# Keys' scores in four tiles that later hold the left tiles' sets; tables spread by products of ones; low parts by GpSimd

## The chip, the cores and the metric

The kernel runs on one core of a Trainium2 chip. A core has a matrix engine (TensorE, here PE, with its weight loads shown apart as PEld), and the engines VectorE (DVE), ScalarE (ACT) and GpSimd (POOL). SyncE (SP) issues most transfers; POOL issues the indirect ones. Each engine takes its instructions in the order in which they were written into its queue. The metric is device time in microseconds, the median of several runs.

## The reference

```python
def _attn_ref(q, k, v, agents):
    scale = 1.0 / np.sqrt(q.shape[-1])
    def sm(a, b):
        s = scale * (a @ b.transpose(0, 2, 1))
        s = s - s.max(-1, keepdims=True)
        e = np.exp(s)
        return e / (e.sum(-1, keepdims=True) + 1e-09)
    a2k = sm(agents, k)
    agent_v = a2k @ v
    q2a = sm(q, agents)
    return q2a @ agent_v
...
    logits = x @ w_gate
    e_idx = np.argmax(logits, axis=1)
...
    for e in range(E):
        mask = e_idx == e
        h = np.maximum(x[mask] @ w1[e], 0.0)
        ye = h @ w2[e]
        out[mask] = gate_w[mask, None] * eom[mask, e, None] * ye
```

q, k and v have shape (4, 11456, 128), and there are 49 agents per batch. The result of the attention, 45824 rows of 128, goes through a layer of 8 experts with 1024 hidden values, each row through the expert of its largest logit. Its output is scaled by that expert's probability and an output gate.

## The kernel before, in words

Each of the 4 batches is cut into 12 units: eleven of 1024 tokens (8 columns of 128) and one of 192. For keys, PE forms scores of a unit against the agents (`ks`), ACT copies them to `S`, DVE keeps a running maximum (`mx`), then POOL subtracts the maximum, ACT takes the exponential (`ev`) and PE adds up the agents' values from `v`.

The output of the attention is never formed for most tokens. The kernel folds the agents' values of a batch into the first weights of the one expert that takes most of this batch's tokens (`fold`, `first`), so that the softmax numerators of q (49 values and their low parts, `x1`, `x2`) are multiplied by 128-row weights `w` at once. This main stream runs over 92 tiles of up to 512 tokens. For each, PE makes eight blocks of hidden values `h` (two groups of four banks), ACT applies the relu and rounds to half precision (`hh`), DVE forms what was rounded away (`hl`), and PE multiplies both by `vv` into `y`. ACT (`ys`) and DVE (`os`) add up `y`, POOL scales it, and SP stores it to `out`.

Scores of q are taken in half precision from high and low parts. `split` makes these: ACT squares the unit for a norm, a product of ones and `scale` give a power of two, ACT writes the high part `xh`, DVE the low part `xl`. The units in `WHOLE` (all keys, the first eight units of batch 0, all of batch 3) are multiplied in single precision instead and pass no split, so 28 units do.

Tokens whose expert is not the batch's main one are the left tokens. Per phase (batches 0 to 2, then batch 3) `q_tail` stores running counts (`cumd`), and `left_table` makes a table of left tiles of 128 tokens: 13 of phase 0, one of phase 1. In this text a left tile is also called a set; `left_index` handles a group of sets at a time: from the table's rows (`tb`, `ti`) and the prefix rows (`pb`) it works out addresses, gathers the counts of `cumd` by indirect transfers on POOL, works out the tokens, and gathers their attention numerators from `efd`. `left_static`, in two interleaved ways, loads the expert's weights, then PE transposes the numerators (`let`), multiplies them by the agents' values (`lx`), and by the two weights in single precision (`lh`, relu, `ly`); `left_scatter` writes over the rows of `out`.

Before the change the tables go through memory: `left_table` stores them (`ttd`, `ttid`, `ppid`), and `left_index` loads them back, spread over all partitions, with a register read on SP for each set. `left_prepare` takes one phase after the other (groups of 2, 3, 3 and 5, then 1); the groups' buffers are the tile of `cum`, two load buffers, and the one tile of `S`, and none is begun before all of batch 3's key weights are summed.

The order of instructions on each queue is made when the program is written: a clock with costs for each operation (`Clock`, `Engine.cost`) decides in which order the generators started with `spawn` are advanced; a smaller second argument is served first. A change of engine or cost in one place thus reorders others. L204 is the line of the helper that writes every instruction.

Of the kernel before, what the change touches and what calls it, by code (L numbers as in the profile page):

```python
# [9 lines left out]
I32 = mybir.dt.int32  # L10
# [243 lines left out]
def agent_attention_top1_moe(ctx, tc, qT, kT, v, aT, wg, wo, w1, w2, cst, out):  # L254
# [158 lines left out]
    def split(item):  # L413
# [3 lines left out]
        while item not in parts or splits[0] - scored_n[0] > 1:  # L417
# [14 lines left out]
                                        op1=ALU.mult)  # L432
        yield from ACT.q.activation(xh[:, 0:n], x[:, 0:n], AF.Copy, scale=s)
        xl = x.bitcast(F16)
        yield from DVE.q.scalar_tensor_tensor(xl[:, 0:n], x[:, 0:n], s, xh[:, 0:n], op0=ALU.mult, op1=ALU.subtract)
# [188 lines left out]
    def k_unit(b, u):  # L624
        if u == 0:
            K[b] = dict(
                S=wk.tile([P, NCOL, A2], F32, name=f"S{b}", tag="S", bufs=1),
                mx=wk.tile([P, 8, A2], F32, name=f"mx{b}", tag="mx", bufs=1),
                sm=wk.tile([P, 8, A2], F32, name=f"sm{b}", tag="sme", bufs=1),
                k=0, s=0, v=0, av_n=0,  # L630
            )
        s, mark, inv = yield from scores(("k", b, u), f"ks{b}_{u}")
        spawn(k_rest(b, u, s, mark, inv))

    def k_rest(b, u, s, mark, inv):
# [5 lines left out]
        Su = S[0:pp, 8 * u:8 * u + nt, :]  # L641
# [5 lines left out]
        if u > 0:  # L647
            yield from DVE.q.tensor_tensor(mx[0:pp, 0:nt], Su, S[0:pp, 0:nt, :] if u == 1 else mx[0:pp, 0:nt],
                                           op=ALU.max)
# [14 lines left out]
    def v_weights(b, u):  # L664
# [3 lines left out]
        sv = S[0:pp, 8 * u:8 * u + nt, :]  # L668
# [572 lines left out]
    def left_table(ph):  # L1241
# [5 lines left out]
        def row(n, w=NG, dt=F32):  # L1247
            return lt(n, [w], f"_{ph}", [min(w, ng)], dt)
# [22 lines left out]
        ppt = lt("pptsb", [P], f"_{ph}", [P])  # L1271
# [15 lines left out]
        ni = a0  # L1287
        yield from DVE.q.tensor_copy(nti[ph], ni[:, ng - 1:ng])

        yield from DVE.q.tensor_scalar(over[:, ph:ph + 1], ni[:, ng - 1:ng], float(PHASES[ph][2]), None, op0=ALU.is_gt)  # L1290
        tt = lt("tt", [4, 8], f"_{ph}", [kr, 8])
# [16 lines left out]
        yield from low_bits(tt[:, :, 3], g_, E - 1, lt("g_i", [4], f"_{ph}", [kr], I32))  # L1308
        yield from DVE.q.tensor_tensor(ne, g_, tt[:, :, 3], op=ALU.subtract)
        yield from DVE.q.tensor_scalar(tt[:, :, 4], ne, 1.0 / E, None, op0=ALU.mult)  # L1310
# [3 lines left out]
        yield from SY.q.dma_start(ttid[ph].rearrange("(k p) c -> p k c", p=P), tti)  # L1314

    def left_index(ph, i, n, nm, got=None, big=None):
# [7 lines left out]
        sl = slice(i, i + n) if isinstance(i, int) else bass.ds(i, n)  # L1324
        yield from SY.q.dma_start(tb.rearrange("p n c -> p (n c)"),
                     ttd[ph][sl, :].rearrange("(o n) c -> o (n c)", o=1).broadcast_to([P, n * 8]))
        yield from SY.q.dma_start(ti, ttid[ph][sl, :].rearrange("(o n) c -> o n c", o=1))
        regs = []
# [4 lines left out]
        for k in range(n):  # L1333
            yield from SY.wait(ti)
            gr = nc.values_load(ti[0:1, k, 0:1], engines=[SP], min_val=0, max_val=ng - 1,
                                skip_runtime_bounds_check_because=WHY)
            yield from SY.q.dma_start(pb[:, k, :], ppid[ph][bass.ds(gr, 1), :].broadcast_to([P, P]))
# [143 lines left out]
    def left_prepare():  # L1481

        for ph, (b0, nb, nst, _) in enumerate(PHASES):
            while counted[0] < b0 + nb:
                yield None
            yield from left_table(ph)
            while B - 1 not in K or K[B - 1]["s"] < NU:
                yield None

            for i, n in [(0, 2), *[(2, 3), (5, 3), (8, 5)]] if nst > 2 else [(0, nst)]:  # L1490
                big = None
                if i > 0 and n <= 3:
                    while not vacant():
                        yield None
                    big = place(("left", ph, i), first_place(0, LARGE)[1], [1024])
                elif i > 0:
                    big = wk.tile([P, NCOL, A2], F32, name=f"big{ph}_{i}", tag="S", bufs=1).rearrange("p t a -> p (t a)")
                def got(k, t, ti, tu, ef, oa):
                    ready[ph, i + k] = t, ti, k, tu[:, k:k + 1], ef[:, k, :], oa[:, k, :]
                yield from left_index(ph, i, n, f"s{ph}_{i}", got, big)  # L1500
# [75 lines left out]
    spawn(left_prepare(), 1)  # L1576
# [72 lines left out]
```

## Time and profile before

| | us |
|---|---|
| median of 3 runs | 1038.69 |
| lowest, highest | 1038.46, 1045.04 |
| the profiled execution | 1040.08 |
| its span | 1038.3 |
| PE busy | 1007.1 |
| DVE, ACT, POOL busy | 838.3, 643.6, 390.3 |
| mean granted clock of PE | 0.994 |

A row of the profile names line, engine, operation, written and read tiles (numbers left out), shape and count; behind the bar stand the busy time in us, the mean of one in ns, and the idle time of the engine ahead of it. An fp32 product shows as two records. The main stream's last product starts at 1010.36 us. Behind it come the last left tiles.

### The profile page before, as it was taken

To read this page: it belongs to the slowest core of one execution; us is meant where nothing else is said; L and a number is where in the kernel's file an instruction comes from. 1 tells how busy PE (TensorE), PEld (TensorE's weight loads), DVE (VectorE), ACT (ScalarE), POOL (GpSimd) and SP (SyncE) were. 2 spreads that over 40 slices of the span, in tenths; PEclk is the share of its full clock that TensorE was granted. 3 is DMA by queue.
4 is the path that set the end of the run, shared out by engine and by line. 5 is a ranking of instruction groups with operands and counts; after the bars stand their busy time and mean duration, and the time that the engine had idled before them with its cause. 6 is when DMAs were issued, how large, how long until landed. Compare 5 with 4: busy or idle time off the path is not lost. (4 is left out here: it accounts for less than half of the span.)

```text
span 1038.3 us, 28383 instructions
## 1 busy us (share of the span) xinstructions
PE 1007.1 (97%) x10927; PEld 814.5 (78%) x10927; DVE 838.3 (81%) x2203; ACT 643.6 (62%) x1489; POOL 390.3 (38%) x692
## 2 busy tenths in 40 slices
PE   9999999999999999999899999999999999999994
PEld 9998777877688778777688778787777678888794
DVE  2648888889889988988979988889998887768740
ACT  2326667676767776766667767666655565565541
POOL 1302445453224364552233454532333334334321
PEclk9999999999999999999999999999999999999997
DMA  7887645463568534545368454436352335343441
GB/s 259 242 241 226 139 144 130 131 153 108 126 170 184 169 122 110 151 120 163 89 181 170 141 134 139 126 120 174 86 97 73 109 101 151 117 150 93 143 140 50
DMA packets 109114, 147.18 MB, mean 142 GB/s; under 512 B 61420, under 2 KB 71840, under 8 KB 108974
## 3 DMA queue, kind: packets, MB, share of 16 engines
q1 hardware_dynamic: 107630, 143.83, 50.1%
q0 software_dynamic: 1344, 1.49, 0.8%
q8 instruction: 87, 1.43, 0.6%
q14 instruction: 53, 0.43, 0.2%
HBM read 91.86 MB, written 35.17 MB: 122 GB/s over the span
## 5 line engine op out<-in xcount | busy, mean ns | idle before, releaser
L204 PE MATMUL y<-vv,hh 128*128 128x256 f16 (+1 forms) x2880 | 584.4, 273 | 10.0 <-DVE os L204 3.2
L204 PE MATMUL y<-vv,hl 128*128 128x128 f16 (+1 forms) x2880 | 530.9, 219 | 3.3 <-DVE hl L204 2.4
L204 DVE SCALAR_TENSOR_TENSOR hl<-h,hh 128x512 f16<-128x512 f32 (+1 forms) x736 | 448.3, 667 | 70.3 <-ACT hh L204 64.1
L204 ACT ACTIVATE hh<-h 128x512 f16<-128x512 f32 (+1 forms) x736 | 373.8, 592 | 202.7 <-PE h L204 200.9
L204 PEld LDWEIGHTS <-hh 128*128 128x128 f16 (+1 forms) x2880 | 282.4, 98 | 56.9 <-issue 31.8
L204 PEld LDWEIGHTS <-hl 128*128 128x128 f16 (+1 forms) x2880 | 313.5, 109 | 17.0 <-issue 8.6
L204 PE MATMUL h<-x_ld,w 128*128 128x512 f16 (+1 forms) x1472 | 276.8, 376 | 2.0 <-DVE hl L204 1.5
L204 PEld LDWEIGHTS <-w 128*128 128x128 f16 x1472 | 93.0, 99 | 89.7 <-issue 67.6
L204 POOL TENSOR_TENSOR os<-os,smt 128x512 f32<-128x512 f32 (+1 forms) x92 | 96.6, 1050 | 131.6 <-DVE os L204 85.1
L204 PE MATMUL av<-ev,v_ld 128*128 128x50 f32 x720 | 110.1, 251 | 0.4 <-ACT ev L204 0.4
L204 PEld LDWEIGHTS av<-ev,v_ld 128*128 128x128 f32 x720 | 107.1, 191 | 2.1 <-ACT ev L204 0.7
L204 PE MATMUL ks<-at,k_ld 128*128 128x50 f32 x720 | 107.6, 255 | 0.0
L204 ACT COPY ys<-y 128x256 f32<-128x256 f32 x180 | 68.3, 380 | 62.2 <-PE y L204 57.9
L204 PEld LDWEIGHTS ks<-at,k_ld 128*128 128x128 f32 x720 | 104.7, 190 | 1.1 <-ACT S L204 0.2
L204 DVE TENSOR_TENSOR os<-y,ys 128x256 f32<-128x256 f32 x180 | 74.6, 416 | 22.0 <-ACT ys L204 20.9
L204 POOL TENSOR_TENSOR ev<-S,km_o 128x400 f32<-128x400 f32 (+1 forms) x44 | 41.0, 933 | 78.2 <-PE av L204 66.5
L204 POOL TENSOR_TENSOR e<-ef,e 128x392 f16<-128x392 f32 (+1 forms) x48 | 42.5, 885 | 65.7 <-ACT e L204 65.2
L204 PEld LDWEIGHTS qs<-at,q_ld 128*128 128x128 f32 (+1 forms) x308 | 47.6, 191 | 2.4 <-DVE os L204 0.5
L204 PEld LDWEIGHTS <-idle_x 128*128 128x128 f16 x325 | 47.7, 153 | 1.7 <-DVE idle_x L204 1.1
L204 PE MATMUL qs<-at,q_ld 128*128 128x50 f32 (+1 forms) x308 | 48.6, 247 | 0.0
L204 POOL TENSOR_TENSOR sm<-sm,ev 128x400 f32<-128x400 f32 (+1 forms) x33 | 41.0, 1242 | 5.3 <-ACT ev L204 4.3
L204 POOL TENSOR_TENSOR ll<-lL,rr 128x128 f32<-128x128 f32 (+1 forms) x48 | 19.0, 396 | 63.1 <-DVE rr L204 36.8
(258 smaller groups left out, 1367.2 us busy)
## 6 DMA issues: line engine op xcount, KB each, us to landing
q_ld<-qT SPq DMA_DIRECT2D x44, 512.0 KB
v_ld<-v SPq DMA_DIRECT2D x44, 512.0 KB
out<-os SPq DMA_DIRECT2D x88, 256.0 KB
k_ld<-kT SPq DMA_DIRECT2D x43, 512.0 KB
lw_ld<-w SPq DMA_DIRECT2D x28, 512.0 KB
efd<-ef SPq DMA_DIRECT2D x44, 200.0 KB
x_ld<-x_ld SPq DMA_DIRECT2D x176, 38.0 KB
w1t<-w SPq DMA_DIRECT2D x8, 256.0 KB
```

The lines of the kernel that those rows point to most:

```text
L204: return getattr(self.eng, op)(*a, **k)
```

## The change

- `split`: the low part is made in two steps. ACT multiplies the unit by the scale in place, and POOL subtracts the high part. Before, DVE did both in one instruction.
- Keys' scores `S`: four tiles of 24, 24, 24 and 18 columns instead of one of 90.
- `left_prepare`: each phase has a generator of its own. Phase 0's sets come in groups of 3, 4, 4 and 2, each group in the tile of the quarter of `S` that it follows, as soon as batch 3's weights of that quarter are summed.
- `left_index`: the table rows and the prefix rows are spread over the partitions by two products with ones instead of transfers. A masked copy is made on DVE ahead of each, and its result is copied from the bank by DVE (`tb`) or ACT (`pb`). The stored tables remain for the loop that takes left tiles over the fixed number.
- `left_table`: prefix sums by one scan instead of doubling steps.

The line of `WHOLE` is the same in both kernels.

Three places in the queues. ACT, where unit 8 of batch 1 is split: `xhq_8` is the high part, `q_8_ld` the unit itself, `ys` the copy of `y`, `hh` the relu. Before:

```order
L204 ACTIVATE hh_7_6845<-h_1_3_6832 128x512
L204 ACTIVATE xhq_8_6768<-q_8_ld,xsq_8_s 128x1024
L204 COPY ys_1_6903<-y_1_6805 128x256
L204 ACTIVATE hh_0_6930<-h_0_0_6915 128x512
L204 ACTIVATE hh_1_6933<-h_0_1_6917 128x512
```

And now:

```order
L204 ACTIVATE ev_0_6777<-ev_0_6777 128x400
L204 ACTIVATE xhq_8_6757<-q_8_ld,xsq_8_s 128x1024
L204 COPY ys_1_6888<-y_1_6819 128x256
L204 ACTIVATE q_8_ld<-q_8_ld,xsq_8_s 128x1024
L204 ACTIVATE hh_0_6912<-h_0_0_6894 128x512
L204 ACTIVATE hh_1_6915<-h_0_1_6899 128x512
```

A second pass over the unit stands between `ys` and the next group of `hh`.

PE, at the end of the main stream (`y` of the last tile, `let`, `lx`, `lh`, `ly` of left tiles, whose number follows the name; 0 is phase 1's). Before:

```order
L204 MATMUL y_0_19746<-vv_1_14310,hl_7_19675 96x128
L204 MATMUL lh_11_1_19824<-lxs_11_19724,lw_110_0_ld 128x128
L204 MATMUL ly_11_19844<-lw_110_0_ld,lh_11_0_19798 128x128 x4
L204 MATMUL ly_11_19844<-lw_110_0_ld,lh_11_1_19837 128x128 x4
L204 MATMUL let_12_19884<-kc,big_8_18061 49x128
L204 MATMUL lx_12_19888<-let_sb_12_19886,lav_12_19813 128x128
L204 MATMUL lh_12_0_19904<-lxs_12_19890,lw_120_0_ld 128x128 x4
L204 MATMUL lh_12_1_19911<-lxs_12_19890,lw_120_0_ld 128x128 x4
L204 MATMUL ly_12_19918<-lw_120_0_ld,lh_12_0_19909 128x128 x2
L204 MATMUL let_0_19921<-kc,bigs_0_19647 49x128
```

And now:

```order
L204 MATMUL y_0_19891<-vv_1_14350,hl_7_19854 96x128
L204 MATMUL let_0_19933<-kc,bigs_0_19379 49x128
L204 MATMUL lx_0_19938<-let_sb_0_19935,lav_0_19861 128x128
L204 MATMUL lh_0_0_19942<-lxs_0_19940,lw_00_0_ld 128x128 x4
L204 MATMUL lh_0_1_19950<-lxs_0_19940,lw_00_0_ld 128x128 x4
L204 MATMUL ly_0_19957<-lw_00_0_ld,lh_0_0_19948 128x128 x4
L204 MATMUL ly_0_19957<-lw_00_0_ld,lh_0_1_19955 128x128 x4
```

The sets 11 and 12 of phase 0 no longer stand behind the last `y`.

DVE, at the indices of phase 1's set (`lrus` is the address for the gather of `cumd`, the instruction with `lppxs` that follows it the first to read what was gathered). Before:

```order
L204 CAST lrus_0_19800<-lrgs_0_19794 128x1
L204 TENSOR_TENSOR bigs_0_19647<-bigs_0_19647,lppxs_0_19783 128x90
L204 TENSOR_REDUCE lccs_0_19842<-bigs_0_19647 128x1
L204 TENSOR_TENSOR os_19838<-y_0_19746,ys_0_19839 96x256
L204 CAST lmis_0_19848<-lccs_0_19842 128x1
```

And now:

```order
L204 CAST lrus_0_19620<-lrgs_0_19612 128x1
L204 TENSOR_TENSOR bigs_0_19379<-bigs_0_19379,lppxs_0_19560 128x90
L204 TENSOR_REDUCE lccs_0_19643<-bigs_0_19379 128x1
L204 CAST lmis_0_19649<-lccs_0_19643 128x1
L204 SCALAR_TENSOR_TENSOR hl_0_19628<-h_0_0_19613,hh_0_19627 128x512
L204 SCALAR_TENSOR_TENSOR hl_1_19631<-h_0_1_19615,hh_1_19630 128x512
```

These instructions have moved ahead of the `hl` of the main stream's last but one tile.

The diff, cut to its core:

```diff
 def split(item):
...
         yield from ACT.q.activation(xh[:, 0:n], x[:, 0:n], AF.Copy, scale=s)
-        xl = x.bitcast(F16)
-        yield from DVE.q.scalar_tensor_tensor(xl[:, 0:n], x[:, 0:n], s, xh[:, 0:n], op0=ALU.mult, op1=ALU.subtract)
+        yield from ACT.q.activation(x[:, 0:n], x[:, 0:n], AF.Copy, scale=s)
+        yield from POOL.q.tensor_tensor(xl[:, 0:n], x[:, 0:n], xh[:, 0:n], op=ALU.subtract)
...
 def k_unit(b, u):
-                S=wk.tile([P, NCOL, A2], F32, name=f"S{b}", tag="S", bufs=1),
+                S=[],
...
 def k_rest(b, u, s, mark, inv):
-        Su = S[0:pp, 8 * u:8 * u + nt, :]
+        if u % 3 == 0:
+            S.append(wk.tile([P, min(24, NCOL - 8 * u), A2], F32, name=f"S{b}_{u}", tag=f"S{u // 3}", bufs=1))
+        Su = S[u // 3][0:pp, u % 3 * 8:u % 3 * 8 + nt, :]
...
 def left_table(ph):
-        t0, t1, t2 = row("t0"), row("t1"), row("t2")
-        yield from DVE.q.tensor_scalar(t0, cnt, 127.0, None, op0=ALU.add)
-        yield from low_bits(t1, t0, 127, row("t1i", NG, I32))
-        yield from DVE.q.tensor_tensor(t0, t0, t1, op=ALU.subtract)
-        yield from DVE.q.tensor_scalar(t0, t0, 1.0 / 128.0, None, op0=ALU.mult)
-        a0, a1 = t0, t2
-        sh = 1
-        while sh < ng:
-            yield from DVE.q.tensor_copy(a1[:, 0:sh], a0[:, 0:sh])
-            yield from DVE.q.tensor_tensor(a1[:, sh:], a0[:, sh:], a0[:, 0:ng - sh], op=ALU.add)
-            a0, a1 = a1, a0
-            sh *= 2
-        ni = a0
+        t0, ni, ti_ = row("t0"), row("t2"), row("t1i", NG, I32)
+        yield from DVE.q.tensor_scalar(ti_, cnt, 127.0, None, op0=ALU.add)
+        yield from DVE.q.tensor_scalar(ti_, ti_, -128, None, op0=ALU.bitwise_and)
+        yield from DVE.q.tensor_copy(t0, ti_)
+        yield from DVE.q.tensor_tensor_scan(ni, ones[:, 0:ng], t0, 0.0, op0=ALU.mult, op1=ALU.add)
+        yield from DVE.q.tensor_scalar(ni, ni, 1.0 / 128.0, None, op0=ALU.mult)
...
 def left_index(ph, i, n, nm, got=None, big=None):
-        for k in range(n):
+        if own:
+
+            tt, ppt = tables[ph]
+            z = c.rearrange("p n k -> p (n k)")[:, 0:8 * n].rearrange("p (n c) -> p n c", c=8)
+            yield from DVE.q.tensor_tensor(z, tt[:, 0, :].unsqueeze(1).broadcast_to([P, n, 8]),
+                                           idf[:, i:i + n].unsqueeze(2).broadcast_to([P, n, 8]), op=ALU.mult)
+            yield from wait_free()
+            t = bank(f"tb{nm}")
+            mark = hold()
+            yield from PE.q.matmul(t[:, 0:8 * n], ones, z.rearrange("p n c -> p (n c)"), start=True, stop=True)
+            yield from DVE.q.tensor_copy(tb.rearrange("p n c -> p (n c)"), t[:, 0:8 * n])
+            release(mark)
+            yield from DVE.q.tensor_copy(ti, tb[0:1])
+            eq = lt("leq", [NSTM], nm, [n])
+            yield from DVE.q.tensor_scalar(eq[0:ng], tb[0:ng, :, 0], pcol[0:ng], None, op0=ALU.is_equal)
+            yield from DVE.q.tensor_tensor(c[0:ng], ppt[0:ng].unsqueeze(1).broadcast_to([ng, n, P]),
+                                           eq[0:ng].unsqueeze(2).broadcast_to([ng, n, P]), op=ALU.mult)
+            yield from wait_free()
+            t = bank(f"pb{nm}")
+            mark = hold()
+            yield from PE.q.matmul(t[:, 0:n * P], ones[0:ng, :], c[0:ng].rearrange("p n k -> p (n k)"), start=True,
+                                   stop=True)
+            yield from ACT.q.copy(pb.rearrange("p n k -> p (n k)"), t[:, 0:n * P])
+            release(mark)
+        else:
...
-    def left_prepare():
-
-        for ph, (b0, nb, nst, _) in enumerate(PHASES):
-            while counted[0] < b0 + nb:
-                yield None
-            yield from left_table(ph)
-            while B - 1 not in K or K[B - 1]["s"] < NU:
-                yield None
-
-            for i, n in [(0, 2), *[(2, 3), (5, 3), (8, 5)]] if nst > 2 else [(0, nst)]:
...
+    def left_prepare(ph):
+
+        b0, nb, nst, _ = PHASES[ph]
+        while counted[0] < b0 + nb:
+            yield None
+        yield from left_table(ph)
+        i = 0
+        for j, n in enumerate((3, 4, 4, 2) if nst > 2 else (nst,)):
+            big = None
+            if nst > 2:
+                while B - 1 not in K or K[B - 1]["s"] < min(3 * j + 3, NU):
+                    yield None
+                big = wk.tile([P, min(24, NCOL - 24 * j), A2], F32, name=f"big{ph}_{i}", tag=f"S{j}", bufs=1)
+                big = big.rearrange("p t a -> p (t a)")
...
-    spawn(left_prepare(), 1)
+    for ph in range(len(PHASES)):
+        spawn(left_prepare(ph), 1)
```

More of the change, by code (lines that the diff above doesn't have):

```diff
@@ L1314, in left_table @@
         yield from SY.q.dma_start(ttid[ph].rearrange("(k p) c -> p k c", p=P), tti)
+        yield from DVE.q.tensor_copy(nti[ph], ni[:, ng - 1:ng])
+        yield from DVE.q.tensor_scalar(over[:, ph:ph + 1], ni[:, ng - 1:ng], float(PHASES[ph][2]), None, op0=ALU.is_gt)
+    tables = {}
     def left_index(ph, i, n, nm, got=None, big=None):
@@ L1323, in left_index @@
         ti = lt("ti" + own, [rows_, 8], nm, [n, 8], I32)[0:1]
[L1324 to L1328, printed above, removed]
         if big is None:
```

43 lines of the change are left out of this document (22 added, 21 removed).

## The prediction

> **What bounds the kernel now.** The page came first, then the waits of the matrix engine (PE).
>
> ```profile
> span 1038.3 us, 28383 instructions
> PE 1007.1 (97%) x10927; PEld 814.5 (78%) x10927; DVE 838.3 (81%) x2203; ACT 643.6 (62%) x1489; POOL 390.3 (38%) x692
> ```
>
> The second row gives each engine's busy time, its share of the span and its instructions. PE is busy for 1007.1 of 1038.3 us, so an edit pays only if it takes work off PE, closes one of its gaps, or shortens the stretch in which PE no longer sets the pace. The waits of PE (total, number of times, longest) say how large the gaps are:
>
> ```profile
> PE let L204 <- issue: 3.8, 1, 3.8
> PE y L204 <- DVE os L204: 3.2, 3, 1.5
> PE y L204 <- DVE hl L204: 2.4, 3, 1.2
> PE y L204 <- ACT S L204: 2.0, 2, 1.6
> ```
>
> The largest single gap, 3.8 us, belongs to the left tiles. The others are waits of the second product `y`, 7.6 us in these rows. The sums by stretch (length, then busy us and instructions of PE, PEld, DVE, ACT, POOL, then granted clock, DMA share, GB/s) show one stretch of the steady part and two of the end:
>
> ```profile
> 300.00:700.00 400.00, 392.72 (x4538) 312.83 (x4536) 358.31 (x883) 279.04 (x632) 170.38 (x304) 1.00 0.53 142
> ...
> 1011.60:1018.45 6.85, 4.31 (x33) 3.63 (x31) 2.69 (x17) 1.97 (x5) 2.79 (x4) 1.00 0.45 152
> 1018.45:1025.28 6.83, 4.72 (x20) 4.30 (x21) 0.00 (x0) 0.89 (x3) 0.04 (x1) 0.57 0.09 30
> ```
>
> In the steady 400 us PE idles 7.3 us; DVE is busy 358.3 (90%), ACT 279.0 (70%). At the end PE works 4.31 of 6.85 us, then at a clock of 0.57. The timeline of the end (start, us, engine, operation, count, idle time before it) says what it waits for:
>
> ```profile
> 1010.36 0.22 PE L204 MATMUL y<-vv,hl 128*96 128x128 f16 x1
> 1010.41 0.44 PE L204 MATMUL lh<-lxs,lw_ld 128*128 128x128 f32 x2
> ...
> 1010.69 2.01 PE L204 MATMUL ly<-lw_ld,lh 128*128 128x128 f32 x16
> ...
> 1012.53 0.27 PE L204 MATMUL let<-kc,big 128*49 128x128 f32 x1
> ...
> 1013.30 0.49 PE L204 MATMUL lx<-let_sb,lav 49*128 49x128 f32 x2 [0.49 <-DVE lfs L204]
> ...
> 1014.14 2.05 PE L204 MATMUL lh<-lxs,lw_ld 128*128 128x128 f32 x16 [0.35 <-ACT lxs L204]
> ...
> 1015.05 1.04 POOL L204 DMA_INDIRECT bigs<-efd,ltu_0s  x1 [0.52 <-POOL bigs L204]
> ...
> 1016.04 0.71 PE L204 MATMUL ly<-lw_ld,lh 128*128 128x128 f32 x4
> 1016.28 0.60 ACT L204 ACTIVATE lh<-lh 128x512 f32<-128x512 f32 x1 [0.30 <-issue]
> ...
> 1020.56 0.42 PE L204 MATMUL let<-kc,bigs 128*49 128x128 f32 x1 [3.81 <-issue]
> ...
> 1027.08 2.07 PE L204 MATMUL ly<-lw_ld,lh 128*128 128x128 f32 x16
> ...
> 1029.23 0.37 ACT L204 ACTIVATE bigs<-ly,bigs 128x128 f32<-128x128 f32 x1 [1.30 <-PEq L1584]
> 1029.87 0.98 POOL L204 DMA_INDIRECT out<-bigs,ltg_0s  x1 [3.63 <-ACT bigs L204]
> ```
>
> The last `y` ends at 1010.58. What is left is the end of phase 0's twelfth set, its thirteenth, and the one set of phase 1. PE meets the latter's `let` in its queue before half of the thirteenth set's `ly`, and stands for 3.81 us until the gather issued at 1015.05 is there. The last scatter starts at 1029.87, and 8.4 us later the span ends. So two sums set the time: PE's work up to the last `y`, and the chain behind it.
>
> **The change part by part.** *The end.* The order shows PE's queue behind the last `y` holding only phase 1's set; the thirteen sets of phase 0 are through before. The chain of one set at full clock comes from the thirteenth: from `let` at 1012.53 to the end of its second relu at 1016.88 is 4.35, then half of an `ly` (2.01 / 2) is 1.0, the scaling copy 0.37 and 0.5 of hand-overs: 6.2 us. Before it PE may wait for the gather: from issue (1015.05) to its `let` (1020.56) it took 5.5 us. In the new order its indices follow the `hl` of the last tile but one, so the last tile's whole work and most of the second product of the one before still cover it; I bound the wait by 0 and 3 us (3.81 was today's) and take 1. From the last `y` to the scatter: 7.2 instead of 1029.87 - 1010.58 = 19.3, **-12.1**. By the Trainium skill, "TensorE: Matmul & The Clock Gate" (Part 1: The HAM clock gate), an idle window of about 3.4 us halves the clock; the row of 0.57 behind a 3.81 us wait agrees, and with a wait of 1 us the chain would stay at 6.2, while at half clock it would be nearer the 9.3 of today's last set (1020.56 to 1029.87).
>
> *The work moved.* What PE did behind the last `y` for phase 0 now stands ahead of it: one product of `lh` (0.25), `ly` 2.01, `let` 0.27, `lx` 0.49, `lh` 2.05, `ly` 2.01, together 7.1; between other products the short ones hide their fill, so **+6.5**.
>
> *The tables by products of ones.* Each of the five groups of sets now spreads its table rows and prefix rows with two fp32 products, new work for PE. The prefix rows of fourteen sets have 128 columns each; eight such products took 2.01 (`ly` above), so 14 x 0.25 = 3.5. The five small products are like the small fp32 products of the gates:
>
> ```profile
> L204 PE MATMUL g<-wgo,avd 128*128 128x16 f32 x8 | 1.2, 230 | 0.0
> L204 DVE SCALAR_TENSOR_TENSOR q_ld<-q_ld,xsq_s,xhq 128x1024 f16<-128x1024 f32 x25 | 34.5, 1379 | 0.4 <-ACT xhq L204 0.4
> L204 ACT ACTIVATE xhq<-q_ld,xsq_s 128x1024 f16<-128x1024 f32 x25 | 29.3, 1173 | 0.0
> L204 POOL TENSOR_TENSOR os<-os,smt 128x512 f32<-128x512 f32 x88 | 93.1, 1058 | 124.0 <-DVE os L204 82.2 <-DVE a L204 14.2 <-DVE t L204 6.9
> ```
>
> (Columns: busy us, mean ns, idle us before. An fp32 product shows as two records.) Four `g` took 1.2 us; five, partly overlapped, cost 1.0. Sum **+4.5**. The transfers that this replaces were off PE:
>
> ```profile
> 988.65 0.35 SPq L204 DMA_DIRECT2D ttd<-tt  x1
> ...
> 1000.35 0.34 SPq L204 DMA_DIRECT2D bigs<-ppid  x1
> ...
> 1005.37 0.28 DVE L204 TENSOR_TENSOR bigs<-bigs,lrs 128x128 f32<-128x128 f32 x1
> ...
> 1008.01 1.07 POOL L204 DMA_INDIRECT bigs<-cumd,lrus  x1 [1.38 <-DVE lrus L204]
> ...
> 1011.41 0.25 DVE L204 TENSOR_TENSOR bigs<-bigs,lppxs 128x90 f32<-128x90 f32 x1 [3.68 <-DMA bigs<-cumd,lrus]
> ```
>
> From the table's store to the first use of the spread rows took 16.7 us for phase 1's set. That goes (two products with a copy each, some 2 to 5 us, stand in its place); it is what lets this set meet the main stream's end, and is paid out in the 7.2 above, not again. The fourteen row fetches and register reads on SP go too; SP releases no large wait of PE in the rows above, so nothing is counted.
>
> *DVE behind the gather.* The last row shows DVE waiting 3.68 us for the gather of `cumd`. Nothing hurried stood behind it. In the new order the four `hl` of the last-but-one tile's first half stand behind that instruction, and their banks hold up PE's next `h`. PE then has the second product of the tile before to work on, about as long as the wait. Cost 0 to 3.7; I take **+1.0**.
>
> *Keys' scores in four tiles.* A group waits only for its own quarter of the last batch's weights. The tables come when batch 2's last units are counted, as before, so this decides where the sets lie, not how much there is: 0. The last batch's scores are whole in both kernels; the words name it, the diff has no line for it: 0.
>
> *The split.* 28 times DVE loses a subtraction (34.5 us for the 25 full ones), ACT gains a copy (like `xhq`, 1173 ns each: 29.3 us) and POOL a subtraction of 1024 elements (twice 1058, so 2.1 us: 53 us). DVE goes from 90% towards 84% in the steady part, ACT from 70 to 76%. None of the three bounds the kernel; PE feels them through its gaps. What a long pass of ACT can do is seen at one place:
>
> ```profile
> 527.52 1.08 ACT L204 ACTIVATE xhq<-q_ld 128x1024 f16<-128x1024 f32 x1
> ...
> 528.56 0.39 ACT L204 COPY ys<-y 128x256 f32<-128x256 f32 x1
> ...
> 529.56 0.27 PE L204 MATMUL y<-vv,hh 128*128 128x256 f16 x1 [1.62 <-ACT S L204]
> ```
>
> `ys`, which frees a bank of `y`, sat behind the split's square, and PE lost 1.62. Such losses are rare: 56 long passes of ACT exist already, and all the waits of `y` above make 7.6. Half as many more costs 0 to 8 (28 x 0.3). Against it, relief of DVE can return at most the idle time that PE has there, 0 to 6 (7.3 per 400 us, not all DVE's). I take **0**, with -6 and +8 for the range.
>
> *Sum:* -12.1 + 6.5 + 4.5 + 1.0 + 0 = -0.1 on the span of 1038.3. The profiled execution took 1040.08, 1.8 more than its span; the median of the three runs is 1038.69. The forecast is 1038.69 - 0.1 = **1038.6**.
>
> **The rivals.** *A, slower: ACT holds the banks of `y`.* Place: the new copy directly in front of `ys` and `hh` on ACT, beside `xhq`. For it: 1.62 above. Against it: PE idles only 7.3 us in 400 with 2 passes per split, and the planner knows the copy's cost. It decides if each of the 28 costs over 0.3: 28 x 0.4 = 11, giving 1050; at 0.2 it is 1044.
>
> *B, DVE is not relieved.* DVE's operations with two operands in SBUF stretch beside POOL (ns min/median/max):
>
> ```profile
> L204 DVE TENSOR_TENSOR oh<-lr,rm x48: 171/224/1039, 90.7 to 946.6; 128x64 f32<-128x64 f32 x44, 96x16 f32<-96x16 f32 x4
> L204 DVE TENSOR_TENSOR mx<-S,mx x40: 245/570/1976, 16.8 to 579.4; 128x400 f32<-128x400 f32 x36, 96x100 f32<-96x100 f32 x4
> ```
>
> The longest `oh` lasts as long as one POOL instruction of 1058. With POOL instructions of 2.1 us, one such wait of half that length per split gives back 28 x 1.05 = 29 of the 37 us, while ACT's load stays: half of A's price, +4, 1043. The Trainium skill, "SBUF — State Buffer" (Who interferes with whom), says that GpSimd and such a DVE instruction lock each other out for a whole instruction; the trace agrees in the 1039.
>
> *C, faster: the relief is real.* PE gets back 6 us in the steady part and the gather is never waited for (-2): 1031.
>
> *D, the sets don't leave the end,* because their gathers or weights come later than planned and PE, which takes its queue in order, stands at a `let` inside the main stream. Against it: none of the thirteen earlier `let` shows in the waits above. Price 13 x 0.5 = 6.5: 1045.
>
> **How the numbers follow.** Forecast 0.45 (1034 to 1043), A 0.17, B 0.15, C 0.15, D 0.08. About 1%, 10.4 us, is what a measurement of this kernel can tell from no change. Only the outer half of A, and D together with A, pass 1049: 0.12. To pass 1028 C would need all the gaps of the steady part: 0.07. The remaining 0.81 is within 1%. The range runs from 1030 (C, a little beyond) to 1047 (B and D, and most of A).
>
> **What the profile will show.** Right: behind the last `y` one `let`, one `lx`, 8 `lh`, 8 `ly`, and 7 us to the scatter; the last `y` near 1022; the new spreads 4 to 5 us of PE; DVE near 84% in the steady part and PE's idle there unchanged. Wrong: a `let` waiting more than 3 us for the gather; `hl` behind the wait for `cumd` with PE idle; waits of `y` for `ys` or `S` far above 7.6 (A); `oh`, `mx`, `a` with means well over those of today (B).

## The result, and the profile after

The changed kernel takes **1051.91 us** (median of 4 runs, 1048.04 to 1053.97), the kernel before, beside it, 1038.58 (1038.33 to 1045.04): a ratio of 1.0107 with a 95% interval of 1.0079 to 1.0135. The forecast was 1038.6 and the range ended at 1047. The profiled execution took 1051.25, its span is 1049.4; against the span before of 1038.3 it is 11.1 longer.

The page of the changed kernel, the span and the busy times:

```profile
span 1049.4 us, 28381 instructions
PE 1014.7 (97%) x10947; PEld 816.4 (78%) x10947; DVE 825.4 (79%) x2178; ACT 671.8 (64%) x1522; POOL 426.6 (41%) x720
```

DVE lost 13 us, ACT gained 28 and POOL 36. The same steady stretch as before, in the sums by stretch (length, then PE, PEld, DVE, ACT, POOL, then granted clock, DMA share, GB/s):

```profile
300.00:700.00 400.00, 388.65 (x4437) 307.41 (x4434) 337.20 (x853) 293.81 (x641) 193.68 (x320) 0.99 0.52 141
```

DVE is at 84% and ACT at 73%, so DVE is relieved. But PE now idles 11.35 us instead of 7.28, and in the same 400 us it starts 4437 instructions where it started 4538. PE's waits of the whole kernel:

```profile
PE h L204 <- DVE hl L204: 6.4, 21, 1.7
PE y L204 <- DVE os L204: 3.7, 5, 1.4
PE y L204 <- DVE w L204: 2.0, 2, 1.5
PE xrq L204 <- ACT xhq L204: 2.0, 1, 2.0
```

The wait of `let` is gone from the list. In its place stands `h` waiting for `hl`, 21 times, in the first product that hardly waited before. The end of the changed kernel, in the timeline:

```profile
1034.99 0.22 PE L204 MATMUL y<-vv,hl 128*96 128x128 f16 x1
1035.04 0.27 PE L204 MATMUL let<-kc,bigs 128*49 128x128 f32 x1
...
1035.82 0.48 PE L204 MATMUL lx<-let_sb,lav 49*128 49x128 f32 x2 [0.51 <-ACT let_sb L204]
...
1036.66 2.05 PE L204 MATMUL lh<-lxs,lw_ld 128*128 128x128 f32 x16 [0.35 <-ACT lxs L204]
...
1038.55 2.01 PE L204 MATMUL ly<-lw_ld,lh 128*128 128x128 f32 x16
...
1041.29 1.04 POOL L204 DMA_INDIRECT out<-bigs,ltg_0s  x1 [4.48 <-ACT bigs L204]
```

Behind the last `y` stands one set alone, and its `let` waits for nothing. From the last `y` to the scatter it is 6.1 us (1041.29 - 1035.21), where it was 19.3. So the end did what it was forecast to do, and the loss lies ahead of the last `y`, which comes at 1035.0 instead of 1010.4. Counting the products `y` one by one in both traces, from 0, number 960 stands at 240.8 (before 240.6), number 1600 at 357.2 (348.5), number 3200 at 611.1 (600.4) and number 4480 at 802.3 (791.9): 10.4 us are lost between 240 and 620 us and nothing for the next 200. GpSimd's 28 subtractions lie between 120 and 661 us. The rest of the 24.6 us by which the last `y` is later is partly the work moved ahead of it and partly a loss near the end, in the same view:

```profile
1016.43 2.06 ACT L204 ACTIVATE hh<-h 128x512 f16<-128x512 f32 x4 [1.94 <-PE h L204]
...
1016.91 1.07 POOL L204 DMA_INDIRECT bigs<-cumd,lrus  x1 [9.32 <-DVE lrus L204]
...
1019.59 0.22 PE L204 MATMUL y<-vv,hl 128*128 128x128 f16 x1
...
1020.17 0.25 DVE L204 TENSOR_TENSOR bigs<-bigs,lppxs 128x90 f32<-128x90 f32 x1 [4.06 <-DMA bigs<-cumd,lrus]
...
1020.81 2.48 DVE L204 SCALAR_TENSOR_TENSOR hl<-h,hh 128x512 f16<-128x512 f32 x4
...
1021.55 0.38 PE L204 MATMUL h<-x_ld,w 128*128 128x512 f16 x1 [1.74 <-DVE hl L204]
1022.15 0.38 PE L204 MATMUL h<-x_ld,w 128*128 128x512 f16 x1 [0.22 <-DVE hl L204]
```

DVE stands 4.06 us for the gather, up to 1020.17, so the four `hl` behind it are late, though the first `hh` that they read was done near 1017.0 (1016.43 and a quarter of 2.06). PE has second products to work on until 1019.81 (1019.59 + 0.22) and then stands for the banks.

### The profile page after: what moved, and what is told of

Same layout as the page of the kernel before. It is cut to its first block, busy times and chain, and to the rows that moved or that the text cites. A ratio compares the mean times of both kernels' runs of the same rounds, so it can differ in the third digit from the quotient of the medians.

```text
span 1049.4 us, 28381 instructions
## 1 busy us (share of the span) xinstructions
PE 1014.7 (97%) x10947; PEld 816.4 (78%) x10947; DVE 825.4 (79%) x2178; ACT 671.8 (64%) x1522; POOL 426.6 (41%) x720
## 5 line engine op out<-in xcount | busy, mean ns | idle before, releaser
L204 POOL TENSOR_TENSOR q_ld<-q_ld,xhq 128x1024 f16<-128x1024 f32 (+1 forms) x28 | 55.1, 1967 | 30.0 <-ACT q_ld L204 29.1
L204 DVE TENSOR_TENSOR mx<-S,mx 128x400 f32<-128x400 f32 (+1 forms) x40 | 26.2, 654 | 22.0 <-ACT S L204 21.8
```

Of the source, the lines that this page charges most:

```text
L204: return getattr(self.eng, op)(*a, **k)
```

## The experiments

Ratios are to the kernel before, run on the same chip as the kernel in question, each with its 95% interval.

### Where does it sit: the split, or the left sets?

**Only the split put back** (changed kernel, old split):

```diff
-        yield from ACT.q.activation(x[:, 0:n], x[:, 0:n], AF.Copy, scale=s)
-        yield from POOL.q.tensor_tensor(xl[:, 0:n], x[:, 0:n], xh[:, 0:n], op=ALU.subtract)
+        yield from DVE.q.scalar_tensor_tensor(xl[:, 0:n], x[:, 0:n], s, xh[:, 0:n], op0=ALU.mult, op1=ALU.subtract)
```

> The changed kernel with the split as before: DVE makes the low part in one instruction, without the second pass of ACT and without POOL's subtraction; all else is the change. Theory S (the split costs PE about 10 us between 240 and 620 us of the span, by the load on ACT and POOL): 1041 to 1043, with the steady part like before, and the late stall behind the gather of cumd (4 to 5 us) still there. Theory R (the loss is the luck of a new order, whatever is moved): anything between 1040 and 1053, with new stalls at other places of the steady part. If the loss sits in the sets and the tables: 1050 to 1052.

Measured: 1043.65 us, ratio 1.0038 (1.0014 to 1.0062). `y` number 4480 stands at 792.0 again, as in the kernel before.

**Only the split** (kernel before, with the two new lines in place of its one):

```diff
-        yield from DVE.q.scalar_tensor_tensor(xl[:, 0:n], x[:, 0:n], s, xh[:, 0:n], op0=ALU.mult, op1=ALU.subtract)
+        yield from ACT.q.activation(x[:, 0:n], x[:, 0:n], AF.Copy, scale=s)
+        yield from POOL.q.tensor_tensor(xl[:, 0:n], x[:, 0:n], xh[:, 0:n], op=ALU.subtract)
```

> The kernel before with the split's three instructions alone changed (second pass on ACT, subtraction on POOL). Theory S: 1048 to 1050, that is about 10 over before, all of it between 240 and 620 us. Theory R: not additive with the run that puts the split back; 1037 to 1050. If the split is free: 1038 to 1040.

Measured: 1047.39 us, 1.0071 (1.0043 to 1.01). The two halves of the change add up within their intervals: 0.0038 + 0.0071 = 0.0109, against 0.0107 for the whole. So the split costs some 7 us, and the left sets some 4.

**The split's two new passes one at a time** (changed kernel; the first with ACT's pass and the subtraction on DVE, the second with the scaling pass on DVE and the subtraction on GpSimd):

```diff
-        yield from POOL.q.tensor_tensor(xl[:, 0:n], x[:, 0:n], xh[:, 0:n], op=ALU.subtract)
+        yield from DVE.q.tensor_tensor(xl[:, 0:n], x[:, 0:n], xh[:, 0:n], op=ALU.subtract)
```

> The changed kernel, but the subtraction of the split is DVE's again, while the second pass stays on ACT; POOL is as before. If ACT's extra pass is what costs: 1050 to 1053. If POOL's 2 us instruction and the lock against DVE is what costs: 1041 to 1044, although DVE has some 30 us more to do than in the changed kernel.

```diff
-        yield from ACT.q.activation(x[:, 0:n], x[:, 0:n], AF.Copy, scale=s)
+        yield from DVE.q.tensor_scalar(x[:, 0:n], x[:, 0:n], s, None, op0=ALU.mult)
```

> The changed kernel, but the scaling pass of the split is DVE's (one operand in SBUF) and the subtraction stays on POOL; ACT is as before. If ACT's extra pass is what costs: 1041 to 1044. If POOL's 2 us instruction is what costs: 1050 to 1053.

Measured: ACT alone 1048.06, 1.0084 (1.0048 to 1.0119); GpSimd alone 1057.58, 1.0175 (1.0123 to 1.0227). Neither pair of expected ranges was met: ACT alone lies between its two, and GpSimd alone beyond both. The form that scales on DVE and subtracts on GpSimd is the slowest of these, though its split takes 14 us less of DVE than in the kernel before (28 passes of a mean of 831 ns instead of 1328).

### The work, or the order that the planner makes of it?

A changed instruction changes the planner's order everywhere. Here the order and the work are told apart, all on the kernel before: a line `planned` puts an instruction into the planner's count without making it.

```diff
+        yield from planned(ACT, "activation", x[:, 0:n], x[:, 0:n], AF.Copy, scale=s)
+        yield from planned(POOL, "tensor_tensor", xl[:, 0:n], x[:, 0:n], xh[:, 0:n], op=ALU.subtract)
+        nc.vector.scalar_tensor_tensor(xl[:, 0:n], x[:, 0:n], s, xh[:, 0:n], op0=ALU.mult, op1=ALU.subtract)
```

> The kernel before, with every queue in the order that the planner makes for the changed split, but with the work of the old split: DVE makes the low part in one instruction, ACT has no second pass and POOL no subtraction. If the new order is what costs (theory R): 1045 to 1049, like the split alone, last y of the steady part (number 4480 of 5760) at 798 to 801 us. If the load costs (theory S): 1038 to 1041, that y at 791 to 794 us.

```diff
+        yield from planned(DVE, "scalar_tensor_tensor", xl[:, 0:n], x[:, 0:n], s, xh[:, 0:n], op0=ALU.mult,
+                           op1=ALU.subtract)
+        nc.scalar.activation(x[:, 0:n], x[:, 0:n], AF.Copy, scale=s)
+        nc.gpsimd.tensor_tensor(xl[:, 0:n], x[:, 0:n], xh[:, 0:n], op=ALU.subtract)
```

> The kernel before, every queue in its old order, but with the work of the new split: second pass on ACT, subtraction on POOL, nothing on DVE. The planner doesn't know of it. Theory S: 1045 to 1050, y number 4480 at 798 to 802 us. Theory R: 1037 to 1041, since DVE is relieved and the order is the old one.

```diff
+        nc.scalar.activation(xh[:, 0:n], x[:, 0:n], AF.Copy, scale=s)
```

> The kernel before in its old order, with the pass that writes the high part made twice on ACT (28 passes more, 30 us); DVE and POOL unchanged. If ACT's extra pass costs by itself: 1043 to 1046. If ACT has room for it: 1038 to 1040.

```diff
+        nc.vector.tensor_scalar(x[:, 0:n], x[:, 0:n], s, None, op0=ALU.mult)
+        nc.gpsimd.tensor_tensor(xl[:, 0:n], x[:, 0:n], xh[:, 0:n], op=ALU.subtract)
```

> The kernel before in its old order, with the low part made by DVE (scaling pass in place, some 0.8 us) and POOL (subtraction, 2 us); ACT unchanged, DVE with some 14 us less. If POOL's long instruction costs by itself, through the waits of DVE for it: 1043 to 1048, with longer means of the instructions of DVE that have two operands in SBUF (oh, a, lr, mx). If not: 1037 to 1040.

Measured: the new order with the old work 1.0058 (1.0033 to 1.0083); the old order with the new work 1.0278 (1.0244 to 1.0311); ACT's pass made twice in the old order 1.0162 (1.0131 to 1.0194); DVE's scaling pass with GpSimd's subtraction in the old order 1.0183 (1.0154 to 1.0213). The three runs in the old order came out 9 to 16 us above the ranges expected of them. Neither theory holds as it was put: the new work costs 29 us in queues that were not planned for it, and planning hides some three quarters of that; but the new order costs 6 us even without the new work. The waits of PE in the run with the old order and the new work show a part of the 29 us:

```profile
PE h L204 <- DVE hl L204: 10.8, 40, 1.9
```

The same wait as in the changed kernel, twice as often.

### The length of one instruction

**Both new passes in halves of 512 elements**, in the changed kernel:

```diff
+        cut = [slice(o, min(o + 512, n)) for o in range(0, n, 512)]
+        for w in cut:
+            yield from ACT.q.activation(x[:, w], x[:, w], AF.Copy, scale=s)
+        for w in cut:
+            yield from POOL.q.tensor_tensor(xl[:, w], x[:, w], xh[:, w], op=ALU.subtract)
```

> The changed kernel with the split's second pass on ACT as two passes of 512 elements, and GpSimd's subtraction as two of 512. The same work, with 28 more instructions of ACT and POOL (about 0.1 us each, 3 us of ACT). Theory L (length: a bank's release waits behind one long instruction in ACT's queue, and DVE behind one long instruction of POOL): what stands in front is half as long, and of the 8 us that the split costs about 4 come back: ratio 1.007. Theory W (work: what counts is how much of ACT's time the planner has to lay beside the chain from h to hh and hl): as the changed kernel, 1.011, or up to 3 us more, 1.014.

Measured: 1.0037 (1.0018 to 1.0055), 7 us faster, though both engines have more instructions and more time (ACT 7.7 us more than in the changed kernel and GpSimd 4.8, where about 3 was expected of ACT). That speaks for length, but the order is another one too. **ACT's pass alone in halves, and GpSimd's alone** (one of the two loops each):

```diff
-        yield from ACT.q.activation(x[:, 0:n], x[:, 0:n], AF.Copy, scale=s)
+        for w in cut:
+            yield from ACT.q.activation(x[:, w], x[:, w], AF.Copy, scale=s)
```

> The changed kernel with only ACT's second pass in two halves of 512; GpSimd's subtraction stays whole (1024 elements, near 2 us). Halving both gave 1.0037, halving none 1.0107. If the length on ACT is the cost (ys, hh and so the banks stand behind it): 1.004 to 1.006. If it is the length on GpSimd (os and the gates' tables behind it, DVE's instructions beside it): 1.009 to 1.011.

```diff
-        yield from POOL.q.tensor_tensor(xl[:, 0:n], x[:, 0:n], xh[:, 0:n], op=ALU.subtract)
+        for w in cut:
+            yield from POOL.q.tensor_tensor(xl[:, w], x[:, w], xh[:, w], op=ALU.subtract)
```

> The changed kernel with only GpSimd's subtraction in two halves of 512; ACT's second pass stays whole (1.08 us). If the length on ACT is the cost: 1.009 to 1.011. If it is the length on GpSimd: 1.004 to 1.006. Both near 1.007 would put half on each.

Measured: ACT's alone 1.0063 (1.0038 to 1.0088), GpSimd's alone 1.0013 (0.9997 to 1.0028). Halves on ACT alone thus gain something too, though their interval overlaps that of the changed kernel (1.0079 to 1.0135); beside halves on GpSimd they gain nothing (1.0037 against 1.0013). **The order of the halves with whole passes in it**, for both passes and then for GpSimd's alone:

```diff
         for w in cut:
-            yield from POOL.q.tensor_tensor(xl[:, w], x[:, w], xh[:, w], op=ALU.subtract)
+            yield from planned(POOL, "tensor_tensor", xl[:, w], x[:, w], xh[:, w], op=ALU.subtract)
+            if w is cut[0]:
+                nc.gpsimd.tensor_tensor(xl[:, 0:n], x[:, 0:n], xh[:, 0:n], op=ALU.subtract)
```

> The queues of e11_halves in the order planned for halves, everything else word for word, but where the first half stands, on ACT and on GpSimd, the whole pass of 1024 is made, and where the second half stands, nothing. Theory L (length of the single instruction): what e11_halves let in between the halves (ys, hh, ev) now waits for the whole pass again: 1.010 or more. Rival O (e11_halves only had a better order of the queues): stays at 1.0037 or, by 28 instructions less on each engine, a little below.

> The queues of e15_pool_halves word for word, but where the first half of GpSimd's subtraction stands the whole of 1024 is made, and where the second half stands, nothing. Theory L (the length of the single GpSimd instruction is what counts): the ratio goes from 1.0013 to 1.006 or more; DVE's sum of busy time, 951.8, goes back towards 960. Theory O (the order of the queues is what counts): it stays at 1.001 to 1.003.

Measured: 1.0067 (1.0043 to 1.009) for both, which is less than theory L said and more than the halves' 1.0037, though the intervals overlap; 1.0088 (1.0057 to 1.0119) for GpSimd's alone, against 1.0013 with halves. In this last pair all queues stand in the same order but for the split's own instruction on GpSimd, and there theory L is met: the length of that one instruction costs 0.0075, 7.8 us. DVE's busy time does not show it: by the sum over all its instructions it went from 951.8 to 953.8, not back to the 960 expected.

The timeline shows how it costs. The run with whole subtractions (L446 is the line that makes them there):

```profile
305.34 2.13 POOL L446 TENSOR_TENSOR q_ld<-q_ld,xhq 128x1024 f16<-128x1024 f32 x1 [4.38 <-ACT q_ld L204]
...
305.65 1.83 DVE L204 SCALAR_TENSOR_TENSOR a<-eo,a 128x8 f32<-128x8 f32 x1
...
307.41 0.55 DVE L204 TENSOR_TENSOR qz<-qs,qm 128x392 f32<-128x392 f32 x1
...
308.02 0.18 PE L204 MATMUL qs<-ah,xhq 128*128 128x50 f16 x1 [2.00 <-DVE qz L204]
```

The same place with halves:

```profile
303.78 2.40 POOL L204 TENSOR_TENSOR q_ld<-q_ld,xhq 128x512 f16<-128x512 f32 x2 [4.37 <-ACT q_ld L204]
...
304.10 0.86 DVE L204 SCALAR_TENSOR_TENSOR a<-eo,a 128x8 f32<-128x8 f32 x1
304.88 0.55 DVE L204 TENSOR_TENSOR qz<-qs,qm 128x392 f32<-128x392 f32 x1
...
305.49 0.18 PE L204 MATMUL qs<-ah,xhq 128*128 128x50 f16 x1 [1.03 <-DVE qz L204]
```

`a` has eight elements per partition. It lasts 1.83 us, until GpSimd's instruction is through, and 0.86 where that one is half as long. `qz` stands behind it, and PE behind `qz`. At this place the clock adds to the price, in the sums of two stretches of 3.4 us of the first run:

```profile
304.80:308.20 3.40, 1.40 (x18) 1.19 (x17) 3.40 (x7) 1.97 (x8) 2.13 (x1) 1.00 0.48 121
308.20:311.60 3.40, 3.40 (x42) 3.01 (x40) 2.03 (x10) 1.32 (x3) 1.66 (x4) 0.50 0.01 2
```

After a stretch in which PE worked 1.40 of 3.40 us, it runs the next 3.4 us at half its clock (0.50), and loses 1.7 more. In the run with halves the clock stays at 1.00 here. The lag of the one run behind the other grows at such places: 3.4 us from 240 to 320, 1.0 near 390, 1.4 from 560 to 590. At each a DVE instruction is held beside a whole subtraction: `lr` for 1.65 us at 253.31 (0.69 with halves), `a` for 1.94 at 388.81, `lr` for 1.65 at 573.45 (0.68) and `km_d` for 2.06 at 583.92 (1.09). The half clock came only at the first of these stretches. The changed kernel has the same thing at the same place, with a `cum` in the part of `a`:

```profile
300.86 3.88 DVE L204 TENSOR_TENSOR_SCAN cum<-ones,oht 128x90 f32<-128x90 f32 x8
...
301.78 2.28 POOL L204 TENSOR_TENSOR q_ld<-q_ld,xhq 128x1024 f16<-128x1024 f32 x1 [2.59 <-ACT q_ld L204]
...
305.71 0.27 PE L204 MATMUL y<-vv,hh 128*128 128x256 f16 x1 [1.39 <-DVE os L204]
```

Four `cum` take 1.04 us in the run with halves, and would take 2.1 for eight; here eight take 3.88, with one of 2.21 among them, and `os`, which frees a bank of `y`, is late. The Trainium skill, "SBUF — State Buffer" (Who interferes with whom), says that of two such instructions, one of GpSimd that reads SBUF and one of DVE with two operands in SBUF, the later blocks until the first is through; the 1.83 and 0.86 agree with it.

### The gather of `cumd`

**The planner counts this gather 4 us longer** (old split put back, so that the steady part is that of the kernel before):

```diff
-            yield from pause(1500.0 if n > 1 else 0.0)
+            yield from pause(1500.0 if n > 1 else 4000.0 if own else 0.0)
```

> The changed kernel with the old split, and with the planner told to count the gather of cumd for phase 1's set 4 us longer, so that the four hl of the last-but-one tile's first half stand ahead of DVE's compare with the gathered rows, and no longer behind it. With the old split alone put back (the run e1_split_back) the ratio to the kernel before was 1.0038, DVE stood 4.07 us for that gather at 1006.92, and PE lost 1.92 + 3 x 0.38 + 1.22 + 2 x 0.26 = 4.8 us behind it. Theory G (this wait is what the tail's part of the change lost): DVE's wait holds no hl, PE's last y ends near 1021.5 instead of 1026, ratio 0.9995 (0.998 to 1.001). Rival: the wait only moves on: the set's second gather is later by the same 4 us, its let then stands 3 to 4 us behind the last y, and the ratio stays at 1.0035.

Measured: 1.0013 (0.9992 to 1.0035), between the two theories. The timeline of the run without the longer count, and of the one with it:

```profile
1011.14 0.25 DVE L204 TENSOR_TENSOR bigs<-bigs,lppxs 128x90 f32<-128x90 f32 x1 [4.07 <-DMA bigs<-cumd,lrus]
...
1012.52 0.38 PE L204 MATMUL h<-x_ld,w 128*128 128x512 f16 x1 [1.76 <-DVE hl L204]
```

```profile
1009.24 0.25 DVE L204 TENSOR_TENSOR bigs<-bigs,lppxs 128x90 f32<-128x90 f32 x1 [0.32 <-DMA bigs<-cumd,lrus]
...
1022.54 0.28 PE L204 MATMUL let<-kc,bigs 128*49 128x128 f32 x1 [2.54 <-DMA bigs<-efd,ltu_0s]
```

DVE's wait fell from 4.07 to 0.32 and PE's last `y` came at 1019.8 instead of 1026.0. Of these 6.2 us 1.9 had been lost before the gather, most of them in a step at half clock at 821.5 that the trace with the longer count does not have. But now the `let` waits 2.54 us for the set's second gather, and the chain behind it runs partly at half clock. By the medians 2.6 us are won, about half of the 4.8 us that PE lost behind the wait; the intervals of the two runs overlap.

### The products, a small change of order, and a version with all of it

**Phase 0's tables spread by transfers again**, on top of the run before:

```diff
-        if own:
+        if own and ph > 0:
...
+            sl = slice(i, i + n) if isinstance(i, int) else bass.ds(i, n)
...
+            for k in range(n):
+                yield from SY.wait(ti)
+                gr = nc.values_load(ti[0:1, k, 0:1], engines=[SP], min_val=0, max_val=ng - 1,
...
+                yield from SY.q.dma_start(pb[:, k, :], ppid[ph][bass.ds(gr, 1), :].broadcast_to([P, P]))
```

> The run e5_back_later, with phase 0's tables spread by transfers as in the kernel before and only phase 1's set by products. PE loses 13 of 14 prefix products of 128 columns (0.25 us each, 3.25) and four of five small ones (0.2 each, 0.8): if the products cost PE their full length, 4 us less than e5_back_later, ratio 0.996 where that one is at 0.9995. Rival: the products lie in gaps that PE has anyway, or SP's register reads and row fetches hold loads up: no less than e5_back_later.

Measured: 0.9987 (0.9966 to 1.0008), 2.7 us less than the run before where 4 were expected; the two intervals overlap.

**One number of the planner**, in the kernel before:

```diff
-    LATE = {"PE": 600.0, "ACT": 0.0, "DVE": 0.0, "POOL": 800.0, "SP": 2000.0}
+    LATE = {"PE": 620.0, "ACT": 0.0, "DVE": 0.0, "POOL": 800.0, "SP": 2000.0}
```

> The kernel before with one number of the planner changed, by which a product is put into PE's queue 620 instead of 600 ns after what it reads is ready by its own count. The work is the same; the queues differ at some hundred rows. In the run e6_order_alone an order planned for the new split, with the old split's work, cost 6.7 us (ratio 1.0058). Theory O (any other order of this planner costs or gains some us: what e6 showed is the scatter between orders): this one differs from the kernel before by 3 us or more either way. Rival (an order planned for the work that it has is as good as another; e6's loss comes from an order that expects passes that are not there): ratio 0.999 to 1.001.

Measured: 0.9994 (0.9972 to 1.0016). This decides little: the number moved only a handful of products, not the order as a whole.

**Halves and transfers together**: with both passes in halves, and with GpSimd's alone. The lines of the second against the changed kernel (the first has ACT's pass in the loop too):

```diff
+        for w in cut:
+            yield from POOL.q.tensor_tensor(xl[:, w], x[:, w], xh[:, w], op=ALU.subtract)
...
-        if own:
+        if own and ph > 0:
...
-            yield from pause(1500.0 if n > 1 else 0.0)
+            yield from pause(1500.0 if n > 1 else 4000.0 if own else 0.0)
```

> The changed kernel with both new passes in halves, phase 0's tables spread by transfers, and phase 1's gather counted 4 us longer. By the sum of the single steps: 1.0037 (halves), -0.0025 (e5_back_later against e1_split_back), -0.0026 (e12_transfers_first against e5_back_later): 0.9986. If DVE's relief is worth something once the passes are short: 0.996.

> The changed kernel with GpSimd's subtraction in halves (as e15_pool_halves, 1.0013), phase 1's gather counted 4 us longer (-0.0025) and phase 0's tables spread by transfers (-0.0026). By the sum 0.996. If the gains don't add up, as in e17_halves_transfers (0.9986 by the sum, 0.9995 measured), 0.998 to 1.001.

Measured: 0.9995 (0.9972 to 1.0018) for the first; the second, with ACT's pass whole, 1035.52 us, **0.9961 (0.9941 to 0.9981)**, as its sum said. It is faster than both kernels, by 4 us against the one before. Its steady part, beside that of the run with whole subtractions (length, PE, PEld, DVE, ACT, POOL, clock, DMA, GB/s):

```profile
300.00:700.00 400.00, 393.75 (x4569) 314.96 (x4568) 339.11 (x874) 301.19 (x655) 200.74 (x344) 1.00 0.54 142
```

```profile
300.00:700.00 400.00, 390.44 (x4500) 310.76 (x4499) 338.42 (x868) 298.30 (x649) 197.91 (x326) 1.00 0.53 143
```

With nearly the same DVE time PE starts 69 instructions more.

## Why the prediction was wrong, step by step

- *The end* (-12.1): right. One `let`, one `lx`, eight `lh` and `ly`, no wait of the `let`; 19.3 became 6.1, so -13.2.
- *The work moved and the tables by products* (+6.5 and +4.5): right in sum. All that PE does ahead of the last `y` in the changed kernel only, priced by the median time from one start to the next (in the trace of before, and of the changed kernel for the new products), comes to some 11. The traces give 9: with the old split the last `y` is 15.6 later than in the kernel before (1025.95 against 1010.36), less the 4.8 behind the gather and the 1.9 lost ahead of it. Of phase 0's products alone the runs give 2.7 instead of 4, with intervals that overlap.
- *DVE behind the gather* (+1.0, bounds 0 and 3.7): the step failed in size, and its upper bound was too low. The wait came as written (4.06 us, `hl` behind it). The cover that was named was there, PE's second products up to 1019.81, but a part of it was already taken: by an estimate from these rows the first `hl` would end near 1017.7 without the wait (its `hh` near 1017.0, and 0.67 for the `hl`), so some 2 us of cover were left for a delay of 3.8 (it begins at 1020.81), and PE stands 1.74. The loss was also counted as the length of the wait at most; the banks then come free one `hl` at a time, so PE stands again and again. Gaps and longer steps between PE's starts, 1.9 + 3 x 0.38 + 1.2 + 2 x 0.26, make 4.8 us, in the run with the split put back and in the changed kernel.
- *Keys' scores in four tiles* (0): nothing in the runs speaks against it; it was not tried alone.
- *The split* (0, bounds -6 and +8): this is the step that decided. It was taken as 0, and the traces with and without it differ by 9.0 us at the last `y` (1034.99 against 1025.95), the runs by 0.0069, 7.2 us. Sums of busy time and a mean idle time of PE could not price it. Rival B named the mechanism, with the price of the average (29 of 37 us given back) and with the wrong sign to look for:

```profile
L204 DVE TENSOR_SCALAR rr<-d,s_s 128x8 f32<-128x8 f32 (+1 forms) x48 | 20.5, 430 | 0.0
L204 DVE TENSOR_TENSOR oh<-lr,rm 128x64 f32<-128x64 f32 (+1 forms) x48 | 16.3, 339 | 0.9
```

These are groups of the changed kernel (busy us, mean ns, idle before). `rr` had a mean of 295 and rose by 6.5 us in all; `oh` had 362 and fell. But the rise of `rr` is no mark of the long subtraction: its mean is 427 with halves too, and 395 in the run that has no subtraction on GpSimd. DVE as a whole really was relieved. What counts is that a single instruction is held for some 2 us (`a` 1.83, `cum` 2.21) when four `hl`, or `os`, or `qz` stand behind it in the queue and PE behind those; the mean of its group does not tell that.
- *Rival A* (ACT holds the banks of `y`): not what happened in the steady part as a whole; but ACT's pass isn't free either. It costs 16.8 us unplanned (1.0162), and with the subtraction left on DVE the planned form stays at 1.0084 against 1.0038. *Rival C* (real relief) may hold once GpSimd's instruction is short: 1.0013 against 1.0038 with the old split, 2.6 us, and `y` number 4480 at 789.5 against 792.0; the intervals overlap. *Rival D*: did not occur.
- The chance of *slower by over 1%* was put at 0.12, since only ACT's price and D could reach it. The split at its bound and the gather beyond its bound, together, did.

Open: no run has the halves in the changed kernel's own order. That the length of GpSimd's instruction costs 0.0075 is shown in the order planned for halves; in the changed kernel's order it is argued from rows like those above, and how the split's 7 us divide there between this length, ACT's pass and the order is not shown. The changed kernel is 2 us slower than the run with whole subtractions in the other order (1.0107 against 1.0088, within their intervals). One more place in it has no part in GpSimd's length:

```profile
532.11 1.06 ACT L204 ACTIVATE xhq<-q_ld 128x1024 f16<-128x1024 f32 x1 [3.01 <-DMA q_ld<-qT]
...
533.31 0.16 PE L204 MATMUL xrq<-xqq,ones 128*128 128x1 bf16 x1 [2.00 <-ACT xhq L204]
```

There a load of `q` comes late to ACT, and PE's next 3.4 us again run at half clock. Whether it is late because the split holds its buffer longer was not tried.

## What to carry to other kernels

A pass moved from DVE to GpSimd is priced by its length and by what stands in DVE's queue behind the instruction that it holds up, not by the busy time that changes hands: try it in pieces before giving the move up (here 1.0013 instead of 1.0088). Ask of every wait that a change adds whether the bounding engine's work that is to cover it already covers something else, and add what is lost while its buffers come back one by one. When an order is planned, run the new work in the old order and the old work in the new one: the two together tell what the plan hides.

## What the runs showed of the hardware

PE's clock falls to half without any stretch of 3.4 us in which PE is idle. In the sums by stretch of the changed kernel 1.78 and 1.40 us of PE's work in 3.40 are followed by 3.4 us at a clock of 0.51 and 0.50; in those of the kernel before, 1.84 is not:

```profile
304.80:308.20 3.40, 1.78 (x16) 1.21 (x15) 3.40 (x8) 0.00 (x0) 0.00 (x0) 0.99 0.46 120
308.20:311.60 3.40, 3.40 (x40) 2.65 (x40) 3.12 (x14) 1.24 (x5) 1.71 (x4) 0.51 0.02 5
...
530.00:533.40 3.40, 1.40 (x15) 0.79 (x14) 0.88 (x4) 1.29 (x3) 1.31 (x2) 1.00 0.90 173
533.40:536.80 3.40, 3.40 (x31) 2.78 (x30) 3.18 (x8) 3.40 (x9) 0.71 (x2) 0.50 0.61 233
```

```profile
528.00:531.40 3.40, 1.84 (x16) 0.92 (x16) 2.27 (x10) 1.62 (x6) 0.54 (x3) 1.00 0.85 237
531.40:534.80 3.40, 3.40 (x50) 3.09 (x48) 2.88 (x6) 3.25 (x6) 0.51 (x2) 1.00 0.59 147
```

The stretches at half clock of one trace lie whole multiples of 3.41 us apart (308.2 and 533.4: 66 of them), so it seems, but is not shown, that PE's work is counted in the steps of a fixed raster: where waits of 2 us or less leave about half of a step or less, the next step costs 1.7 us on top. That is not the whole rule: near 820 us several runs show a slow step behind one in which PE was busy for 0.78 of it, and in the changed kernel PE works 1.71 of 3.40 us from 1018.10 to 1021.50, a step of the same raster, and the next step stays at 1.00. Each of these is one execution.
